# An S4 convolution block with a GEGLU block on one core: first spectrum table on another queue, two activation tables called early, one wider product, and a new order of all steps

## The chip, the cores and the metric

The kernel runs on one core of a Trainium2 chip. The metric is the device time of one execution in microseconds. Before the change it is 791.32 us, the median of 3 runs (790.24 to 792.32).

## The reference, cut to what matters

A sequence of 2048 tokens with 448 channels passes two blocks. The first is a state-space convolution: from the complex parameters A, B, C (448 channels by 256 states) a kernel K of 2048 taps is generated for each channel, and the normalized input is convolved with it. The second is a gated feed-forward block (GEGLU) of width 1792. Both have a layer norm modulated by rows of `silu(c) @ w_mod`.

```python
mod = (_silu(c) @ w_mod).reshape(c.shape[0], 6, 1, -1)       # sa, ca, ga, sb, cb, gb
h = _layernorm(x) * (1 + ca) + sa
# _A_ref: dt = exp(log_dt);  P = exp(dt * A * l);  K = Re(sum_n C * P * dt * B)
#         y = irfft(rfft(K) * rfft(h))[:L] + h * Dskip
x = x + ga * _A_ref(h, ...)
h = _layernorm(x) * (1 + cb) + sb
x = x + gb * (gelu(h @ w_gate) * (h @ w_up)) @ w_down
```

## The kernel before, in words

**Preparation of the taps.** The function `prep(t)` turns 112 channels of A, B and C into two small tables: the logarithm of the magnitude of C*B*dt and of its exponent per tap (`l0`), and the phase (`l1`). It does so in some twenty steps, named `p.A1` to `p.S4` in the code, on [112, 256] tiles. A logarithm (Ln, line 569), an exponential (line 570) and an arctangent (line 580) are among them, all on ScalarE (ACT). Each table is split into three bf16 pieces (`pieces`, lines 527 to 538), written to DRAM (`put`, line 595) and read back transposed in stages of 56 channels (`load_lt`, line 620), tiles `lt`. Tables `ea` and `rd` hold tap numbers. `prep` runs four times, the stage loop eight times.

**Generation.** For each group of 8 channels (`s` = 0 to 55), TensorE (PE) multiplies `lt` with `rd` or `ea` (lines 638, 657, 675), ACT takes exponentials (`mx` line 644, `my` line 662), sines and cosines (`fg`, lines 688, 692, 699), VectorE (DVE) multiplies them (`tx` line 721, `ty` line 725), and PE sums over the states (`kgen`, line 748). Exponentials, sines, logarithm, arctangent and square root each need an activation table in ACT, and an `ACT_TABLE_LOAD` stands in ACT's row wherever the table changes.

**Convolution.** The input is normalized in blocks of 512 tokens (`xt`; statistics lines 877 and 878, scaling line 904) and transformed (`ua` line 921, `ub` line 984) into spectra `us`, kept in DRAM. `k_fft` transforms 160 channels of K at a time, in 11 batches of frequencies: forward product on PE (line 1094, PSUM tile `pf`), product with two u spectra on DVE (lines 1097 and 1098, 3 x 160 elements each; the second spectrum is the first with its halves exchanged), inverse on PE (line 1105). The last 128 channels go through `t_fft`.

**Modulation rows.** `mod_row` (line 800) loads a row of `w_mod` (784 KB) into a buffer of the ring `fg`, which has 4 buffers and also serves the sines, and multiplies it with silu(c) on PE (lines 811 and 815). Three rows are needed at the start, three later.

**Feed-forward block.** Four blocks of 512 tokens: convolution result and norm (`conv_out`), gate and up products (line 1530), down products (lines 1599 and 1630), in fp16 pairs.

**What sets the order.** Every step is a task with a number in the table `PLACE`. The tasks are emitted in the order of these numbers, so each engine's row of instructions, and each DMA queue's, follows from the table. A letter behind a number (a, d, s, p) picks ACT, DVE, SP or POOL where a step can run on several. An engine takes its row strictly in order. SP issues most DMAs; a DMA also waits for the completion of the one eight issues before it, since eight semaphores take turns. In the kernel before, ACT issues the first loads of A, B and C (line 511 for `t` = 0), the two writes of the first table (line 595) and its four reads (line 620). Buffers: 4 of tag `q` for `prep` and `k_fft`, 4 `fg`, 9 `my`, 5 `mx`, 2 `lt`, 2 PSUM tiles `pg`.

Of the kernel before, what the change touches and what calls it, by code (L numbers as in the profile page):

```python
# [40 lines left out]
    "anc": "120 138 145 163 157 200 209 244 266 311 327 339 347 355 438 456 470 487 499 524",  # L41
    "ang": "108 112 126 149 151 169 204 212 241 298 319 324 341 350 421 443 454 476 496 506 511 591 602 610 654 670 690 698 "
        "741 761 764 775 792 795 805 885 894 905 908 927 932 950 1007 1018 1021 1034 1039 1051 1115 1124 1135 1151 1157 1169 "
        "1187 1197",
    "as": "67d 80a 99d 109d 114d 128d 156a 185a 250d 258d 265a 289d 309d 333d 334d 365d",
    "bn": "48 49 60 58 41 50 51 53 227 243 235 239 187 224 197 210",
    "c.ai": "1257",
    "c.ak": "5",
    "c.au": "4",
    "c.c": "2",  # L50
    "c.ea": "20",
    "c.ih": "1283",
    "c.ld": "7",
    "c.rd": "22",
    "c.t1": "219",
    "co.adde": "1329 1347 1366 1355",
    "co.addl": "1384 1387 1421 1410",
    "co.addx": "1495 1510 1499 1522 1676 1716 1739 1688 1799 1811 1817 1809",
    "co.ca": "1404a 1408a 1456a 1441a",
    "co.cb": "1415d 1416a 1459a 1448a",  # L60
    "co.h0": "1398a 1403a 1447d 1430a",
    "co.h2": "1534a 1579a 1571a 1561a 1752a 1748d 1759a 1765d 1856d 1889a 1841a 1873a",
    "co.l0": "1402 1405 1449 1434",
    "co.l2": "1541 1584 1573 1576 1753 1754 1763 1766 1857 1893 1851 1884",
    "co.mme": "1321 1341 1336 1346",
    "co.mml": "1381 1382 1409 1407",
    "co.mmx": "1492 1506 1494 1509 1640 1703 1735 1649 1792 1805 1812 1796",
    "co.n": "1392 1399 1438 1425",
    "co.nx": "1527 1574 1548 1532 1749 1746 1751 1764 1829 1875 1837 1870",
    "co.rc": "1390 1397 1431 1423",  # L70
    "co.rcx": "1525 1743 1828",
    "co.rt": "1388 1393 1424 1418",
    "co.rtx": "1524 1741 1818",
    "co.xt": "1541 1584 1573 1576 1753 1754 1763 1766 1857 1893 1857 1884",
    "co.ta": "1401 1406 1453 1436",
    "co.tb": "1411 1413 1454 1439",
    "cos": "523 609 623 635 689 694 715 708 760 774 794 791 804 819 817 893 906 912 930 946 949 963 1016 1028 1040 1050 1057 "
        "1066 1129 1134 1155 1175 1180 1196 1207 1220",
    "cos2": "124 146 147 167 165 207 213 254 273 321 332 342 349 359 445 462 485 492 502 531",
    "d.hi": "1566 1547 1583 1496 1533 1600 1504",  # L80
    "d.ld": "1555 1538 1569 1484 1516 1585 1491",
    "d.lo": "1567 1552 1587 1501 1535 1602 1514",
    "d0": "13",
    "dn": "1603 1605 1607 1613",
    "dn.k0": "1742 1891 1994",
    "dn.k2": "1755 1896 2000",
    "dn.k3": "1757 1899 2002",
    "dn.r": "1606 1608 1614 1634",
    "dn.r1": "1745 1963 2008",
    "dn.r4": "1768 1903 2004",  # L90
    "dn.r5": "1770 1909 2010",
    "dn.r6": "1778 1908",
    "dn.rh": "2005 2012 2016",
    "dn.s0": "2015",
    "dn.s1": "2017",
    "dn.st": "1657 1658 1620 1639 1747 1780 1775 1779 2007 1952 1950 1948 2014 2006 2013",
    "dn0": "1726 1737 1880 1885 1986 1992",
    "dn1": "1738 1887 1993",
    "dn2": "1767 1902 2003",
    "dn3": "1772 1905",  # L100
    "dn3h": "2009 2011",
    "dn4": "1750 1897 1999",
    "dn5": "1744 1894 1998",
    "dn6": "1761 1898 2001",
    "dsk": "178",
    "dt": "26",
    "e.f": "1666 1718 1704 1615 1650 1628 1685",
    "e.hi": "1668 1720 1708 1617 1653 1631 1689",
    "e.ld": "1656 1705 1696 1610 1638 1619 1675",
    "e.lo": "1671 1723 1710 1618 1655 1636 1691",  # L110
    "ev.end": "1253",
    "ev.fp": "707",
    "ev.geg": "1445",
    "ev.pq": "1328",
    "ev.ps": "1437",
    "ev.ub": "389",
    "ev.w0": "1339",
    "f.fc": "714 716 754 773 801 823 851 880 895 917 942 1015 1030 1052 1071 1094 1114 1137 1158 1189",
    "f.fwd": "738 753 783 806 832 855 879 902 924 947 969 998 1014 1036 1055 1077 1098 1120 1141 1162 1209 1216",
    "f.inv": "750 768 796 815 847 865 889 911 936 960 983 1010 1026 1046 1067 1089 1108 1130 1154 1176 1226 1232",  # L120
    "f.pr": "743 759 790 812 839 859 884 907 931 953 975 1002 1020 1041 1060 1083 1101 1125 1149 1167 1212 1225",
    "f.st": "763 782 809 830 897 878 904 929 977 1000 1009 1023 1042 1079 1090 1106 1131 1148 1168 1193 1243 1240",
    "f.ut": "710 721 755 776 803 826 854 870 901 918 944 966 988 1017 1032 1054 1073 1097 1123 1138 1160 1182",
    "f.z": "758a 778d 802a 829a 868a 871d 896d 926a 952d 979a 1005d 1019a 1038d 1061a 1085a 1102a 1128d 1143a 1163a 1188a "
        "1235a 1239a",
    "gs": "70 110",
    "gu": "1480 1497 1511 1519 1528 1539 1549 1560 1570 1578 1596 1616 1622 1632 1644 1651 1660 1669 1678 1686 1694 1706 "
        "1712 1721 1777 1781 1784 1798 1800 1808 1816 1822 1830 1838 1843 1852 1859 1869 1907 1910 1913 1919 1924 1931 1935 "
        "1941 1945 1958 1964 1970 1974 1981",
    "gu.g": "1429 1450 1458 1465 1468 1471 1474 1481 1502 1508 1521 1529 1540 1550 1562 1572 1581 1595 1604 1623 1633 1641 "  # L130
        "1654 1661 1670 1679 1687 1695 1709 1713 1722 1727 1782 1785 1793 1801 1806 1813 1824 1831 1839 1844 1853 1860 1874 "
        "1878 1911 1914 1920 1925 1932 1936 1942 1946 1959 1965 1972 1975 1982 1987",
    "gu.h0": "1475 1485 1515 1536 1557 1580 1599",
    "gu.ha": "1626 1647 1663 1682 1698 1717 1730 1787 1804 1819 1835 1849 1864 1882 1917 1933 1943 1953 1967 1977 1989",
    "gu.hs": "1629 1646 1667 1690 1701 1732 1734 1794 1820 1826 1846 1862 1871 1888 1923 1930 1955 1957 1983 1979 1996",
    "gu.l0": "1478 1488 1517 1544 1558 1582 1601",
    "gu.la": "1635 1648 1672 1684 1700 1725 1733 1789 1825 1834 1855 1854 1866 1883 1918 1939 1956 1961 1968 1984 1990",
    "gu.ls": "1630 1652 1673 1693 1702 1740 1736 1797 1821 1840 1850 1865 1872 1890 1929 1940 1971 1960 1995 1980 1997",
# [16 lines left out]
    "lt0": "55 136 317 358 568 766 860 955",  # L155
    "lt1": "87 173 335 393 696 833 971 995",
    "m.cp": "532d 589a 818d",
    "m.cp0": "40d",
    "m.ev": "63 68 47 545 598 838",
    "m.ld": "6 19 12 423 539 727",  # L160
    "m.mm": "45 57",
# [1672 lines left out]
```

## Time and profile before

| what | value |
|---|---|
| median of 3 runs | 791.32 us (790.24 to 792.32) |
| the profiled execution's own time | 787.92 us |
| its span, first to last instruction | 786.1 us |
| PE busy | 728.7 us (93%) |
| DVE busy | 591.4 us (75%) |
| ACT busy | 460.1 us (59%) |
| POOL busy | 9.0 us |
| mean granted clock of PE | 0.991 |
| DMA, mean over the span | 178 GB/s |

The span is cut into 40 slices of 19.65 us in the page; a digit is the busy share of a slice in tenths. A row of a timeline has its start, its duration, the engine, the source line, the operation, the tile written and the tile read; in brackets stands how long the engine was idle before it, and what it waited for. Names such as SPq and ACTq stand for an engine's sequencer, which issues DMAs beside the engine's arithmetic. Line numbers are those of the kernel before; the changed kernel's are higher by 2 from line 434 on, by 4 from `prep` on, by 5 behind its arctangent, and by 4 again behind line 1097.

### The profile page before, as it was taken

The numbers are of one execution on the slowest core, as the hardware profiler recorded it, in microseconds if no ns is written. First come the engines' busy times: TensorE is split into PE (matmuls) and PEld (weight loads), VectorE is DVE, ScalarE is ACT, GpSimd is POOL, SyncE is SP. The second block draws the span as 40 slices with busy tenths as digits, with TensorE's granted clock in tenths as the row PEclk, the third lists the DMA queues.
The fourth block names the chain that finished last, engine by engine and source line by source line (L and its number), as shares of the span: only waits on it lengthen the run. The fifth ranks groups of instructions, "written<-read, shape, count | busy, mean of one in ns | idle before, by whom it ended". The sixth has DMA issues, their size and how long they took to land.

```text
span 786.1 us, 19037 instructions
## 1 busy us (share of the span) xinstructions
PE 728.7 (93%) x8166; PEld 445.2 (57%) x8166; DVE 591.4 (75%) x891; ACT 460.1 (59%) x613; POOL 9.0 (1%) x24
## 2 busy tenths in 40 slices
PE   1876889998899999989999999999999999999998
PEld 0333454543667767778784445444595446944478
DVE  4889999999999999988768851469773587134743
ACT  5699999899999999961554730233421244012320
POOL 0000000000000000000300000000000000000000
PEclk9899999999999999999999999999999999999999
DMA  9555558997887767999797884345437324012201
GB/s 265 157 156 145 155 140 249 277 277 227 240 259 216 224 190 216 285 300 251 192 312 221 274 219 146 129 134 186 161 67 213 104 94 134 14 48 94 82 2 60
DMA packets 103791, 139.88 MB, mean 178 GB/s; under 512 B 34388, under 2 KB 85268, under 8 KB 103706
## 3 DMA queue, kind: packets, MB, share of 16 engines
q1 hardware_dynamic: 97828, 130.47, 56.7%
q10 hardware_dynamic: 5318, 7.22, 2.9%
q8 instruction: 64, 1.05, 0.5%
q0 software_dynamic: 560, 0.98, 0.4%
q14 instruction: 21, 0.17, 0.1%
HBM read 100.39 MB, written 36.01 MB: 174 GB/s over the span
## 4 chain that ended last, share of the span: by engine, by line
PE 67%; ACT 13%; DVE 9%; DMA 7%; issue 3%; SPq 1%; ACTq 0%; DVEq 0%
PE pq L1530 29%; PE pq L1630 9%; PE pd L1599 4%; PE kg L748 3%; PE pf L1105 3%; PE pg L675 3%; ACT my L662 2%; DVE ty L725 2%; PE pf L1094 2%; ACT fg L688 2%; PE pq L1524 2%; PE kg L771 2%; DMA yi<-y 2%; PE pd L1630 2%; PE pf L984 1%
## 5 line engine op out<-in xcount | busy, mean ns | idle before, releaser
L1530 PE MATMUL pq<-ht,wr 128*128 128x512 f16 (+1 forms) x1200 | 248.3, 365 | 0.1
L1530 PEld LDWEIGHTS <-wr 128*128 128x128 f16 x1200 | 114.7, 98 | 128.4 <-issue 11.3
L725 DVE TENSOR_TENSOR ty<-my,fg 128x2048 f32<-128x2048 f32 x56 | 127.6, 2285 | 0.9 <-ACT fg L699 0.3
L1537 ACT ACTIVATE ge<-pq 128x512 f32<-128x512 f32 (+1 forms) x60 | 33.9, 566 | 106.4 <-PE pq L1524 71.2
L1544 DVE TENSOR_TENSOR fq<-ge,pq 128x512 f32<-128x512 f32 (+1 forms) x60 | 39.0, 649 | 73.0 <-PE pq L1530 46.1
L1556 ACT ACTIVATE hh<-fq 128x1024 f16<-128x1024 f32 (+1 forms) x49 | 46.7, 961 | 63.9 <-DVE fq L1544 45.3
L721 DVE TENSOR_TENSOR tx<-mx,fg 128x1024 f32<-128x1024 f32 x56 | 67.7, 1219 | 1.8 <-ACT fg L692 1.0
L1630 PE MATMUL pq<-d,hh 128*128 128x224 f16 x476 | 68.9, 259 | 0.0
L748 PE MATMUL kg<-ty,tx 128*32 128x64 f32 x3584 | 62.5, 221 | 4.0 <-issue 2.3
L748 PEld LDWEIGHTS kg<-ty,tx 128*32 128x32 f32 x3584 | 53.0, 110 | 22.7 <-issue 14.7
L1559 DVE TENSOR_TENSOR hlo<-fq,hh 128x1024 f16<-128x1024 f32 (+1 forms) x49 | 53.7, 1106 | 12.9 <-ACT hh L1556 12.7
L1630 PE MATMUL pq<-d,hlo 128*128 128x224 f16 x238 | 61.6, 259 | 0.0
L688 ACT ACTIVATE fg<-pg 128x1024 f32<-128x1024 f32 x56 | 58.1, 1038 | 0.8 <-PE pg L675 0.4
L662 ACT ACTIVATE my<-pg 128x1024 f32<-128x1024 f32 x56 | 55.9, 1032 | 2.6 <-PE pg L657 2.2
L1630 PEld LDWEIGHTS <-hh 128*128 128x128 f16 x560 | 54.2, 98 | 0.9 <-issue 0.2
L1105 PE MATMUL pf<-q,fc 128*128 128x160 f32 x264 | 41.5, 307 | 1.2 <-DVE q L1098 1.2
L692 ACT ACTIVATE fg<-fg,small 128x1024 f32<-128x1024 f32 x36 | 41.5, 1170 | 0.1
L1105 PEld LDWEIGHTS pf<-q,fc 128*128 128x128 f32 x264 | 36.4, 190 | 6.6 <-issue 1.5
L675 PEld LDWEIGHTS <-lt 64*128 64x128 bf16 x304 | 17.9, 95 | 39.0 <-issue 27.0
L675 PE MATMUL pg<-ea,lt 64*128 64x512 bf16 x152 | 30.7, 391 | 8.4 <-ACT fg L699 3.2
L1747 ACT ACTIVATE d<-fq 128x896 f16<-128x896 f32 x14 | 13.2, 946 | 41.7 <-PE pd L1599 27.3
L984 PE MATMUL pf<-ui,fu 128*128 128x448 f32 x66 | 31.0, 575 | 1.9 <-ACT uo L480 1.4
(209 smaller groups left out, 1122.6 us busy)
## 6 DMA issues: line engine op xcount, KB each, us to landing
wr<-w_d SPq DMA_DIRECT2D x21, 896.0 KB
fc<-in_k_fc SPq DMA_DIRECT2D x20, 576.0 KB
u_d<-so SPq DMA_DIRECT2D x32, 224.0 KB
ui<-u_d SPq DMA_DIRECT2D x10, 672.0 KB
fq<-in_wd SPq DMA_DIRECT2D x14, 448.0 KB
w<-in_wgu SPq DMA_DIRECT2D x11, 512.0 KB
us<-uo SPq DMA_DIRECT2D x22, 240.0 KB
q<-us SPq DMA_DIRECT2D x22, 240.0 KB
```

The costliest lines, as they stand in the source:

```text
L662: A.activation(yb.tile.rearrange("p h (n k) -> p n h k", n=2), pb.tile.rearrange("p (n h k) -> p n h k", n=2, h=2), AF.Exp)
L675: T.matmul(pa[:, nh * 512:nh * 512 + 512], w, x, start=(k == 0), stop=(k == 2))
L688: A.activation(fb.tile[:, 0].rearrange("p x (n k) -> p n x k", n=2), pb.tile.rearrange("p (n x k) -> p n x k", n=2, x=2), AF.Sin, scale=TW ...
L692: A.activation(fb.tile[:, 1], fb.tile[:, 1], AF.Sin, scale=-TWO_PI, bias=halfpi)
L721: V.tensor_mul(tx.tile, xb.tile[:, xm, None, :].to_broadcast([128, 2, 512]), fb.tile[:, :, 0])
L725: V.tensor_mul(ty.tile, yb.tile[:, :, None, :].to_broadcast([128, 2, 2, 512]), fb.tile[:, None, :, 1].to_broadcast([128, 2, 2, 512]))
L748: T.matmul(kg[32 * g:32 * g + 32, 2 * (s % 2) + q, :64], tx[:, r, nh, 4 * q + g], ty[:, 0:4:3, nh, 4 * q + g] if r else ty[:, 1:3, nh, 4 * ...
L1105: T.matmul(pz.tile[:, e % 32 - sl0], fc.tile[:, i, 1 + t], pp.tile[:, t, i], start=(t == 0 and e != 32), stop=(t == 1 and e != 0))
L1530: T.matmul(pb.tile[k][:, ts], wr.tile[:, 4 * lo + t, k, c0:c0 + 128], ht[:, m, ts], start=f % 2 == 0 and i == 0, stop=f % 2 == 1 and i == 9)
L1556: A.activation(hg.tile[0][:, cb, c], fq.tile[:, c], AF.Copy)
L1559: V.tensor_sub(hg.tile[1][:, cb, c], fq.tile[:, c], hg.tile[0][:, cb, c])
L1630: T.matmul(bank(k)[:, m], x[:, p, q[0], ts], w[:, p, q[1]], start=new and m == 0 and p == 0 and z == 0, skip_group_check=True, stop=i in ( ...
```

## The change

It has five parts.

1. The writes and reads of the first table (`put`, `load_lt` for the first stage) are issued by SP and no longer by ACT.
2. In `prep` the logarithm is written to `x(7)`, not over `x(10)`. It so no longer waits for the load of the second half of A, B, C (`L3` is the buffer of that load). The step `p.B2` reads `x(7)`, and `p.E1`, which overwrites `x(7)`, now waits for `p.B2`.
3. Two one-element activations are added, a logarithm behind the first exponential (`pre.ln`) and an arctangent behind the step `p.S3` of the first `prep` (`pre.at`). The table loads that belong to them stand there in ACT's row.
4. In `k_fft` one DVE instruction multiplies both u spectra with the K spectrum, which is read twice by a broadcast: 22 instructions of 960 elements in place of 44 of 480.
5. `PLACE` has new numbers for all tasks.

```diff
-    "c.ld": "7",
+    "c.ld": "8",
...
+    PRE_LN = add("pre.ln", {"ACT": 0.2}, -8.4, lambda: A.activation(dump, eps, AF.Ln), [t_dt], table=LN)
...
-        S2 = op("S2", {"ACT": 0.28}, lambda: A.activation(x(10), x(3), AF.Ln), [B1, L3], LN, k=0.6)
-        S3 = op("S3", {"ACT": 0.28}, lambda: A.activation(x(2), x(10), AF.Exp, scale=0.5), [S2], EXP, k=0.65)
+        S2 = op("S2", {"ACT": 0.28}, lambda: A.activation(x(7), x(3), AF.Ln), [B1, PRE_LN if t == 0 else None], LN, k=0.6)
+        S3 = op("S3", {"ACT": 0.28}, lambda: A.activation(x(2), x(7), AF.Exp, scale=0.5), [S2], EXP, k=0.65)
...
+        pre_at = add("pre.at", {"ACT": 0.2}, v0, lambda: A.activation(dump, eps, AF.Arctan), [S3], table=ATAN) if t == 0 else None
...
-        B2 = op("B2", {"ACT": 0.28}, lambda: A.activation(x(10), x(10), AF.Identity, scale=0.5, bias=ld[:, t:t + 1]), [S2, S3], k=0.7)
+        B2 = op("B2", {"ACT": 0.28}, lambda: A.activation(x(10), x(7), AF.Identity, scale=0.5, bias=ld[:, t:t + 1]), [S2, L3], k=0.7)
...
-        S4 = op("S4", {"ACT": 0.28}, lambda: A.activation(x(5), x(5), AF.Arctan), [D1], ATAN, k=1.0)
+        S4 = op("S4", {"ACT": 0.28}, lambda: A.activation(x(5), x(5), AF.Arctan), [D1, pre_at], ATAN, k=1.0)
...
-        E1 = op("E1", {"DVE": 0.66}, phase, [S4, G1], k=1.1)
+        E1 = op("E1", {"DVE": 0.66}, phase, [S4, G1, B2], k=1.1)
...
-                (adma if t == 0 else dma)(lh_d[t, e, :, :6], lb.tile)
+                dma(lh_d[t, e, :, :6], lb.tile)
...
-                (adma if sc == 0 else dma)(
+                dma(
...
-            for t in range(2):
-                V.tensor_mul(pp.tile[:, t, :ne], ut.tile[:, t, :ne], pk.tile[:, :ne])
+            V.tensor_mul(pp.tile[:, :, :ne], ut.tile[:, :, :ne], pk.tile[:, None, :ne].to_broadcast([128, 2, ne, n]))
```

What the new numbers do is seen in the rows of the engines. The first place is SP's queue at the start of the program, before (`xt` are the input tokens, `ld` and `c_sb` the small vectors log_dt and c, `fg` a row of w_mod, `q` the parameters A, B, C of the next `prep`, `au` and `ak` stage matrices):

```order
1 L486 DMA c_sb<-in_c 112x4
2 L486 DMA au<-in_k_au 128x128
3 L486 DMA ak<-in_k_ak 128x256
4 L805 DMA fg<-in_w_mod 112x1792
5 L486 DMA ld<-in_A_log_dt 112x4
6 L852 DMA xt<-in_A_u 128x1792
7 L805 DMA fg<-in_w_mod 112x1792
8 L852 DMA xt<-in_A_u 128x1792
9 L805 DMA fg<-in_w_mod 112x1792
10 L486 DMA ea<-in_k_ea 128x1536
11 L486 DMA rd<-in_k_rd 128x1025
12 L511 DMA q<-in_abc 112x1024
```

The same place in the changed kernel:

```order
1 L857 DMA xt<-in_A_u 128x1792
2 L488 DMA ld<-in_A_log_dt 112x4
3 L488 DMA c_sb<-in_c 112x4
4 L810 DMA fg<-in_w_mod 112x1792
5 L857 DMA xt<-in_A_u 128x1792
6 L810 DMA fg<-in_w_mod 112x1792 x2
7 L600 DMA lh_d<-lh 112x1536
8 L488 DMA au<-in_k_au 128x128
9 L488 DMA rd<-in_k_rd 128x1025
10 L515 DMA q<-in_abc 112x1024
11 L625 DMA lt<-lh_d 64x7x128 x2
12 L488 DMA ea<-in_k_ea 128x1536
```

The first block of tokens now comes first, the write of the first table (`lh_d`) stands ahead of `au`, `rd`, the next parameters and `ea`, its two first reads (`lt`) ahead of `ea`, and `ak` comes later than is shown.

The second place is ACT's row at the start, before (`small` is a column of constants; the rows of line 511 are DMAs that ACT issues):

```order
1 L511 DMA q<-in_abc 112x1024
2 L511 DMA q<-in_abc 112x512
3 L551 ACT_TABLE_LOAD
4 L551 ACTIVATE q<-q 112x512
5 L552 ACTIVATE q<-q 112x256
6 L569 ACT_TABLE_LOAD
7 L569 ACTIVATE q<-q 112x256
8 L570 ACT_TABLE_LOAD
9 L570 ACTIVATE q<-q 112x256
10 L577 ACTIVATE q<-q,ld 112x256
11 L494 ACTIVATE dts__106<-ld 112x4
```

and in the changed kernel:

```order
3 L496 ACT_TABLE_LOAD
4 L496 ACTIVATE dts__106<-ld 112x4
5 L497 ACTIVATE dts__106<-dts__106 112x4
6 L500 ACT_TABLE_LOAD
7 L500 ACTIVATE small<-small 128x1
8 L568 ACTIVATE q<-q,dts__106 112x256
9 L569 ACTIVATE q<-q 112x256
10 L555 ACTIVATE q<-q 112x512
11 L556 ACTIVATE q<-q 112x256
12 L573 ACTIVATE q<-q 112x256
13 L582 ACTIVATE q<-q,ld 112x256
14 L797 ACT_TABLE_LOAD
```

The exponential of log_dt (`dts`), which needs the vector `ld`, moved from behind the logarithm to the front of the row, the table of the logarithm is loaded behind it, and the logarithm itself (line 573) has no table load of its own any more; the table of exponentials is loaded again behind it.

The third place is DVE's row at the start of the changed kernel; before, the product of line 542 (now 546) was the first row behind the two memsets:

```order
3 L882 BN_STATS st<-xt 128x6
4 L883 BN_AGGR mv<-st 128x2
5 L882 BN_STATS st<-xt 128x6
6 L883 BN_AGGR mv<-st 128x2
7 L546 TENSOR_TENSOR q<-q 112x1024
8 L551 TENSOR_TENSOR q<-q 112x256
9 L552 TENSOR_TENSOR q<-q 112x256
```

Two blocks of token statistics moved ahead of the first product of A, B and C.

Counted over all rows of the phase of generation, the letters in the table move single steps between ACT and DVE. To DVE go three bf16 pieces (`lh`), one copy of a K spectrum's rows (`ako`) and two further copies; to ACT go three copies of `zo` of 480 elements, three copies of `ke`, one absolute value of 1024 elements (`fg`) and one further copy. ACT has 42 table loads in place of 43, and two added activations of one element. In the feed-forward block four splits of `hl` (two instructions each) move from ACT to DVE.

The three later loads of w_mod rows stand at 462, 564 and 749 in the table (423, 539 and 727 before), and their products on PE at 503, 576 and 773 (527, 581 and 772 before).

More of the change, by code (lines that the diff above doesn't have):

```diff
@@ L594, in go @@
             def go():
-                (adma if t == 0 else dma)(lh_d[t, e, :, :6], lb.tile)
-            return add("p.put%d" % e, {"ACT" if t == 0 else "SP": 0.42}, v0 + dv * k, go, dep, use=[lb], kb=344)
+                dma(lh_d[t, e, :, :6], lb.tile)
+            return add("p.put%d" % e, {"SP": 0.42}, v0 + dv * k, go, dep, use=[lb], kb=344)
         PUT[t] = (put(0, l0, [P0], 1.1), put(1, l1, [P1], 1.7))
@@ L619, in go @@
             for nh in range(2):
-                (adma if sc == 0 else dma)(
+                dma(
                     b.tile[64 * nh:64 * nh + 64, e],
                     lh_d[t, e, c0:c0 + 8 * SUBS, :, 128 * nh:128 * nh + 128].rearrange("(s c) q n -> (c q) s n", c=8))
-        q = {"ACT": 1.3} if sc == 0 else {"SP": 0.9}
+        q = {"SP": 0.9}
         e0 = add("lt0", q, v, lambda: go(0), [PUT[t][0], PAD[t]], [b], kb=299)
```

440 rows, old and new, of the table PLACE are left out of this document.

## Prediction

> **What bounds the kernel now.** I read the page's busy slices first, then a table by stage, then the chain of waits and the timeline of the first 46 us.
>
> ```profile
> span 786.1 us, 19037 instructions
> PE   1876889998899999989999999999999999999998
> DVE  4889999999999999988768851469773587134743
> ACT  5699999899999999961554730233421244012320
> ```
>
> The kernel has three parts. In the first two or three slices no arithmetic engine is full. Up to slice 17 DVE and ACT are both full, with PE close behind. From slice 18 on PE is full to the end. The table by stage gives sizes; its columns are PE, PEld, DVE, ACT and POOL busy, the granted clock, the DMA engines' share and GB/s.
>
> ```profile
> 0.00:20.00 20.00, 2.55 (x9) 0.73 (x10) 9.85 (x24) 10.60 (x18) 1.52 (x11) 1.00 0.91 263
> 20.00:40.00 20.00, 16.32 (x50) 7.65 (x50) 17.17 (x39) 13.13 (x19) 0.00 (x0) 0.87 0.55 163
> 60.00:80.00 20.00, 13.08 (x272) 7.35 (x271) 19.76 (x33) 19.90 (x26) 0.00 (x0) 0.98 0.51 149
> 120.00:140.00 20.00, 18.43 (x275) 8.82 (x276) 19.84 (x27) 17.52 (x28) 0.00 (x0) 1.00 0.88 248
> 320.00:340.00 20.00, 18.39 (x469) 13.34 (x472) 20.00 (x19) 18.65 (x24) 0.00 (x0) 1.00 0.96 300
> 480.00:500.00 20.00, 20.00 (x108) 10.18 (x106) 5.49 (x10) 0.95 (x1) 0.00 (x0) 1.00 0.07 20
> ```
>
> In the first 40 us ACT lacks 16.3 us and DVE 13.0 us of work. From 60 to 340 us each is between 88 and 100% busy in the stages shown, so time there is saved only by work taken off them or by better packing. In the last part PE shows no gap: what the change moves there (four splits of `hl`) lies beside PE's work and costs nothing while PE has 20.00 of 20; if that cover were gone, four splits would be about 2 us, each a cast like `lh` below (0.41) and a small one. So the change is decided at the start and in the generation.
>
> The chain of waits says what the start waits for, and gives the price of transfers.
>
> ```profile
> 0.75 4.65 DMA q<-in_abc
> 18.52 7.48 DMA lh_d<-lh
> 97.35 3.25 DMA u_d<-so
> 121.03 8.37 DMA fg<-in_w_mod
> ```
>
> The parameters land at 5.4 us, `prep` runs to 18.5, and the write of the first table then takes 7.48 us. A write of 224 KB in a later, quieter stage takes 3.25. The difference is explained by the DMA engines, which are full from about 3 us until 25 us:
>
> ```profile
> 6.00:8.00 2.00, 0.00 (x0) 0.00 (x0) 1.41 (x3) 1.28 (x2) 0.00 (x0) 1.00 1.11 310
> 24.00:26.00 2.00, 2.00 (x5) 0.98 (x5) 1.97 (x5) 0.63 (x1) 0.00 (x0) 1.00 0.71 275
> ```
>
> **Part by part: the start.** These are the rows of the timeline on which the first term rests.
>
> ```profile
> 5.42 1.22 DVE L542 TENSOR_TENSOR q<-q 112x1024 f32<-112x1024 f32 x1 [4.51 <-DMA q<-in_abc]
> 7.47 0.63 ACT L551 ACTIVATE q<-q 112x512 f32<-112x512 f32 x1 [0.72 <-DVE q L548]
> 9.17 1.28 ACT L569 ACT_TABLE_LOAD   x1 [0.76 <-DVE q L558]
> 10.46 0.42 ACT L569 ACTIVATE q<-q 112x256 f32<-112x256 f32 x1
> 13.10 1.75 DVE L574 RECIPROCAL q<-q 112x256 f32<-112x256 f32 x1
> 16.44 1.72 PE L811 MATMUL pf<-fg,c_sb 112*32 112x448 f32 x8 [16.44 <-DMA fg<-in_w_mod]
> 20.79 8.13 PE L815 MATMUL pf<-fg,c_sb 112*128 112x448 f32 x16
> 26.09 1.36 ACTq L620 DMA_DIRECT2D lt<-lh_d  x2
> 28.85 0.09 PEld L638 LDWEIGHTS <-lt 64*128 64x128 bf16 x1 [0.65 <-DMA lt<-lh_d]
> 31.26 1.02 ACT L644 ACTIVATE mx<-pg 128x1024 f32<-128x1024 f32 x1
> 43.66 1.02 ACT L688 ACTIVATE fg<-pg 128x1024 f32<-128x1024 f32 x1
> ```
>
> The mark that I follow is the first exponential of the generation, at 31.26, and the first sine, at 43.66.
>
> *Arrival.* ACT's first step now waits for `ld`, which stands behind 896 KB of `xt` on SP's queue, and DVE's first step waits for `xt` itself. At best they land as the parameters do now, at 5.4. At worst they wait for all of the first loads, 896 KB of tokens, 672 KB of parameters and 224 KB of ones: 1792 KB at 310 GB/s is 5.9 us, from about 2 us on, so 7.9. I take 7.0, between the two and nearer the late end.
>
> *Chain of the first table.* ACT: `dts` 0.4, table of the logarithm 1.28, the dummy 0.2, line 564's two steps 0.9, ready at 9.8. DVE: two token statistics at about 0.8 (0.615 below and a short aggregate), then 2.1 for lines 542 to 548 as now (5.42 to 7.47): 10.7. Squares, sizes and the logarithm took from 7.47 to 9.17 and then 0.42; without the table load the logarithm ends at 12.8. Then line 577 (0.5), the table of exponentials 1.28, two small steps 0.6: 15.2, where it is 12.6 now (10.46, 0.42, another load of 1.28 and 0.42). The three steps around the reciprocal take 2.6: 17.8. The arctangent table lies under them, so the arctangent follows at once and takes 0.4, to 18.2. The bf16 pieces of the first table need the tail of ACT's row and two subtractions, 2.2 together: the write is issued at about 20.0 (17.8 and 2.2), 1.5 us later than now.
>
> *What it meets.* At 18.52 the write finds ahead of it the parameters, ones, two token blocks, three w_mod rows, and besides them `au`, `ak`, `ea`, `rd` and the next parameters, 1280 KB in all, at 310 GB/s worth 4.1 us. Of these all but `ak`, which comes much later, now stand behind it. 7.48 less 4.1 is 3.4, close to the quiet 3.25. So I take 3.3 and the write lands at 23.3, not 26.0. The reads follow with the 2.76 us that they take now (26.09 to 28.85), plus 0.5 for `au`, `rd` and parameters that go between: 26.6.
>
> *What comes last then.* ACT must first bring in the modulation rows and the square root. PE's chain for the rows starts when silu(c) is there, about 16.1 (16.44 now); 4.1 (half of 8.13), 1.7, 4.1 and 1.0 for the sum over rows (two of the sixteen) give 27.0, then one copy of 0.5 and a table load of 1.28: the first exponential at 28.8 in place of 31.26, **2.5 us earlier**. Here PE's chain and no longer the table comes last, which is why the 2.25 us by which the table is early and the loads of the two tables are not all kept. ACT's own stand on the reads (at 26.09, and the wait ahead of it) is gone, since SP now holds them; queued behind SP's waits are the next parameters and `ea`, and `ea` is needed only at the second kind of product of the stage. The second table, which ACT reads now behind its first exponentials, goes the same way and is earlier too, so it doesn't hold the sine: I carry 2.5 us to the first sine. Ends: 4 if the first loads land at 5.4, 0.5 if the chain of the first table is 2 us later than worked out.
>
> The Trainium skill, page "DMA: Bandwidth & Descriptors", section "Issuing engines are not separate DMA queues", says that DMAs from all issuing engines run on the same 16 DMA engines and interleave, and that issuing from several saves only issue time. By this rule the change of queue alone leaves the write at 7.48 us, and only the order of what stands ahead can help; the full DMA shares above agree with it, and it speaks for the first rival.
>
> The skill's page "ScalarE: Activation LUTs", section "What ACT_TABLE_LOAD costs", gives 1283 ns for the load and a drain of about 1380 ns more. The rows show 1.28 us and the logarithm 0.01 us behind it, so no drain; by the page a load that is taken off the path would be worth 2.66 us.
>
> **Part by part: the generation.** These groups carry the second term (busy us, mean ns).
>
> ```profile
> L725 DVE TENSOR_TENSOR ty<-my,fg 128x2048 f32<-128x2048 f32 x56 | 127.6, 2285 | 0.9 <-ACT fg L699 0.3 <-ACT fg L692 0.3 <-issue 0.2
> L721 DVE TENSOR_TENSOR tx<-mx,fg 128x1024 f32<-128x1024 f32 x56 | 67.7, 1219 | 1.8 <-ACT fg L692 1.0 <-ACT fg L699 0.9
> L1098 DVE TENSOR_TENSOR q<-q,pf 128x480 f32<-128x480 f32 x44 | 26.7, 648 | 1.2 <-PE pf L1094 1.0
> L877 DVE BATCH_NORM_STATS2 st<-xt 128x6 f32<-128x448 f32 x16 | 9.8, 615 | 0.0
> L683 DVE TENSOR_SCALAR fg<-pg 128x1024 int32<-128x1024 int32 x6 | 7.3, 1220 | 0.9 <-PE pg L675 0.9
> L680 ACT ACTIVATE fg<-pg 128x1024 f32<-128x1024 f32 x30 | 30.8, 1035 | 0.9 <-DVE ke L766 0.7
> L482 DVE COPY zo<-pf 128x480 f32<-128x480 f32 x7 | 4.6, 653 | 0.5 <-PE pf L1105 0.5
> L480 ACT ACTIVATE zo<-pf 128x480 f32<-128x480 f32 x13 | 7.6, 588 | 0.0
> L482 DVE COPY ke<-kg 128x252 f32<-128x252 f32 x17 | 7.0, 412 | 0.2
> L480 ACT ACTIVATE ke<-kg 128x252 f32<-128x252 f32 x11 | 4.3, 393 | 4.1 <-PE kg L748 4.1
> L482 DVE CAST lh<-q 112x512 bf16<-112x512 f32 x7 | 2.8, 412 | 0.0
> L480 ACT ACTIVATE lh<-q 112x512 bf16<-112x512 f32 x9 | 5.8, 639 | 6.6 <-DVE q L589 2.4 <-DVE q L536 2.4 <-DVE sig L795 1.8
> ```
>
> *The product.* Lines 721 and 725 differ by 1024 elements and 1066 ns, so 1.04 ns an element; 960 elements would take 1219 less 64 x 1.04, 1152 ns. Two of 480 take 26.7/22 = 1.21 us of DVE. That is 0.06 us for each of 22 batches, 1.4 us in all.
>
> *The letters.* ACT: three pieces less (-1.92), three `zo` (+1.76), three `ke` (+1.18), one `fg` (+1.04), two copies less and one more (-0.6), one table load less (-1.28), two dummies (+0.4): 0.6. DVE: +1.24 -1.96 -1.24 -1.22 and about +0.7 for the copies: -2.5, with the product -3.9. ACT gets nothing off and DVE 3.9 of some 290 us. Since either engine can come last, a stretch gains only where DVE does. I take **1.0 us** of the 3.9; the ends are -1 (ACT last throughout) and 3.9.
>
> *The new order* in this stretch has no row that prices it. ACT lacks 2.5 us in the stage from 120 to 140, where a w_mod row sits in one of four `fg` buffers from 121.03 until its product (104 steps of the table later; now 41). A shorter stay can give up to 2.5 back, and other waits can come; I take nothing, with 3 us either way as an estimate from that one stage's shortfall.
>
> **The sum.** Against the profiled execution's own 787.92: 787.9 - 2.5 - 1.0 = 784.4. It lies 3.4 us under the median of 791.32, so against the runs I say 791.3 - 3.5 = **787.8 us**.
>
> **The rivals.** A difference below 0.3%, 2.4 us, can't be told from no change here.
>
> *The start is given back.* The engines become full 2.5 us earlier, but a later transfer sets the pace, so the first stall, such as the stage from 120 us on, takes up the gain. For it: the DMA share is 0.88 to 0.96 there, and these bytes are not fewer. Against it: DVE is at 19.84 in that stage, so what is done ahead of it counts. It gives 789 to 793, say 790.5.
>
> *The later w_mod rows hold PE up*, the rival on the other side. The loads for the second and the third late row stand only 12 and 24 steps ahead of their products in the table. Step 423 was reached at 121.03, so a step is 0.286 us: leads of 3.4 and 6.9 us against 8.37 that such a load took. PE would stand 5.0 + 1.5 = 6.5 us, ACT and DVE starve behind it, since PE's row is strict and the two `pg` buffers cover only about 2 us. Less the 3.5 gained that is 3.0 slower, 794.3. It decides when SP issues the load less than 8.4 us ahead of the product. Against it: SP has nothing else to do and may run ahead of the table.
>
> *More than forecast.* The shorter stay of the first row gives its 2.5 us back and DVE's 3.9 count in full: 2.5 + 3.9 + 2.5 = 8.9, 782.4.
>
> *The change doesn't do what it says*: the logarithm's table could be loaded twice if another function came between; ACT's row in the order shows none. The middle of this is the first rival's time.
>
> **How the numbers follow.** Forecast 0.45, more 0.12, given back 0.25, PE held up 0.18. Faster by over 0.3% takes the forecast without the share in which the start yields under 2.4 (0.02), and "more": 0.55. The same: 0.02 + 0.25 = 0.27. Slower: 0.18. The range leaves out a part of "more" and of the held-up case: 783.0 to 794.0.
>
> **What would show it.** Right: the first exponential near 28.8 and the first sine near 41.2; the write of the first table landing near 23.3; the logarithm without a table load ahead of it; line 1102 with 22 instructions near 1.15 us; all stages after the start earlier by a growing amount, up to about 3.5 us where the gate products begin. Wrong: the first exponential later than 30.5 (the loads land late), ACT or PE idle for over 2 us in front of a product of `fg` and `c_sb`, or gate products that begin no earlier than now.

## The result, and the profile after

The changed kernel takes 795.84 us (median of 16 runs, 790.38 to 802.60), the kernel before 789.56 (16 runs, 786.29 to 792.32). The ratio is 1.0086, 95% interval 1.0068 to 1.0104: **slower by 0.86%**, where I forecast 787.8 us. The ratio leaves out the run of 802.60 us, the only one in a slow state, and is not the quotient of the two medians (1.0080). The profiled execution of the changed kernel took 792.80 us (span 791.0) and lies 3.0 us under its median, that of before took 787.92 and lies 1.6 under its own. So the two profiles differ by 4.9 us and the runs by 6.3: the profile shows the loss a little too small.

These are the slices of the changed kernel's page. PE has an 8 and a 7 in slices 20 and 22 (376 to 396 and 415 to 435 us), where it had 9, and ends on 7 in place of 8.

```profile
PE   1776889999999999999897999999999999999997
DVE  5899999999999999979665853378872787135653
ACT  5699999999999999943542730143421342013320
```

**The start.** The timeline of the changed kernel, DVE's first statistic, ACT's first step, the write and the reads of the first table on SP, PE's first use of the table, the first exponential and the first sine; below them a row of the table by 2 us (PE, PEld, DVE, ACT, POOL, clock, DMA share, GB/s):

```profile
7.59 0.63 DVE L882 BATCH_NORM_STATS2 st<-xt 128x6 f32<-128x448 f32 x1 [6.68 <-DMA xt<-in_A_u]
9.30 0.21 ACT L496 ACTIVATE dts__106<-ld 112x4 f32<-112x4 f32 x1 [6.34 <-DMA ld<-in_A_log_dt]
21.40 0.32 SPq L600 DMA_DIRECT2D lh_d<-lh  x1
24.31 1.35 SPq L625 DMA_DIRECT2D lt<-lh_d  x2
30.11 0.28 PE L643 MATMUL pg<-rd,lt 64*128 64x256 bf16 x1 [2.75 <-DMA lt<-lh_d]
31.02 2.86 ACT L649 ACTIVATE mx<-pg 128x1024 f32<-128x1024 f32 x3 [1.78 <-PE pg L643]
43.06 1.94 ACT L693 ACTIVATE fg<-pg 128x1024 f32<-128x1024 f32 x2
...
20.00:22.00 2.00, 2.00 (x5) 0.97 (x3) 1.97 (x5) 1.31 (x3) 0.00 (x0) 1.00 0.00 0
```

The first exponential is at 31.02, not at the forecast 28.8 (31.26 before), the first sine at 43.06 (43.66 before). From the write's issue to the reads' issue it is 2.9 us now, where it was 7.57 (18.52 to 26.09). But from the reads' issue to PE's first use 5.8 us pass, where 2.76 passed, and PE waits 2.75 us. The last row shows why that need not be: from 20 to 22 us no DMA moves at all. SP stands at the table's write, and behind it in SP's row stand `au`, `rd` and the next parameters (768 KB, issued from 21.76 to 22.80) and `ea` (issued at 25.71), which then run into the write and the reads.

**The generation.** The merged product has the length that I worked out (1152 ns). The first product of the last transforms marks the generation's end, the first row of before, the second of the changed kernel:

```profile
354.78 1.60 PE L1189 MATMUL pf<-ako,fc 128*128 128x128 f32 x12 [0.70 <-ACT ako L480]
```

```profile
L1102 DVE TENSOR_TENSOR q<-q,pf 128x960 f32<-128x960 f32 x22 | 25.2, 1147 | 2.4 <-PE pf L1099 2.4
...
349.35 1.60 PE L1193 MATMUL pf<-ako,fc 128*128 128x128 f32 x12 [0.70 <-ACT ako L482]
```

It ends 5.4 us earlier in this execution. That is more than the 3.5 that I forecast for start and generation together, though the start gave nearly nothing (0.24 us at the first exponential, 0.6 at the first sine).

**Behind the generation** the gain is lost and more. PE's waits from 340 us to the end, the longest of before and then of the changed kernel:

```profile
PE pd L1409 <- DMA yi<-yb_d: 1.0, 1, 1.0
...
PE pd L1409 <- DMA yi<-y: 0.4, 1, 0.4
```

```profile
PE pd L1413 <- DMA yi<-y: 4.0, 1, 4.0
PE pd L1413 <- DMA y<-lh: 2.8, 1, 2.8
PE pq L1694 <- DVE xn L1701: 2.3, 1, 2.3
```

There are three places. In order of time they are the wait of 2.8 us (at 378 us, for block 0's `yi`), that of 4.0 (at 416 us, for block 1's `yi`) and that of 2.3 (at 781 us, for the last block's half result). PE's timeline shows what they cost; before first, then the changed kernel:

```profile
392.44 2.34 PE L1530 MATMUL pq<-ht,wr 128*128 128x256 f16 x20
...
418.58 0.44 PE L1409 MATMUL pd<-yi,ai 128*64 128x128 f32 x4 [0.36 <-DMA yi<-y]
...
420.04 4.49 PE L1530 MATMUL pq<-ht,wr 128*128 128x512 f16 x20
...
431.08 8.81 PE L1530 MATMUL pq<-ht,wr 128*128 128x512 f16 x40
```

```profile
389.54 2.35 PE L1534 MATMUL pq<-ht,wr 128*128 128x256 f16 x20
...
419.78 0.70 PE L1413 MATMUL pd<-yi,ai 128*64 128x128 f32 x4 [3.96 <-DMA yi<-y]
420.23 1.31 PE L1408 MATMUL pd<-yi,ai 128*64 128x320 f32 x4
...
422.44 5.48 PE L1534 MATMUL pq<-ht,wr 128*128 128x512 f16 x20
...
434.48 8.81 PE L1534 MATMUL pq<-ht,wr 128*128 128x512 f16 x40
```

The gate products begin 2.9 us early (389.54 against 392.44), so 2.5 of the 5.4 went in the transition up to there; the longer first wait (2.82 against 1.04 us) is 1.8 of them. Forty products of 512 columns behind the second wait the same work begins 3.4 us late (434.48 against 431.08): 6.3 us went there. Of these the longer wait is 3.6 us, and 2.2 go by between its end and the last row, at a lower granted clock: twenty gate products take 5.48 us where they took 4.49, and the first `yi` products 0.70 where they took 0.44. About 0.9 comes back until 760 us, and the third wait takes 2.4: -5.4 + 2.5 + 6.3 - 0.9 + 2.4 = +4.9, the difference of the spans.

*Why `yi` of block 1 is late.* The chain of waits of the changed kernel names the store that it waits for, and ACT's queue what stands ahead of that store:

```profile
396.50 13.14 DMA y<-zo
410.38 9.27 DMA yi<-y
```

```profile
395.56 0.85 ACTq L1363 DMA_DIRECT2D w_d<-wr  x2
...
396.50 0.52 ACTq L1235 DMA_DIRECT2D y<-zo  x1
```

Two stores of split weights (`wr.sa`, 896 KB each) go out together, right ahead of the last stores of `y`. Before, the first went out at 388.42 and the second at 396.34, behind ACT's last `y` at 393.83. ACT's is not the only late store: POOL's last `y`, which waits for DVE's `zo`, is issued at 399.20 (393.26 before) and takes 10.3 us, so both land near 409.6. No run here moves POOL's store alone. The table of stretches (before, then changed) shows the rest:

```profile
388.00:396.00 8.00, 7.42 (x75) 5.87 (x74) 7.72 (x21) 6.22 (x13) 0.69 (x1) 1.00 0.91 301
396.00:416.00 20.00, 20.00 (x177) 15.42 (x176) 12.26 (x26) 11.31 (x20) 0.00 (x0) 1.00 1.01 287
416.00:424.00 8.00, 7.64 (x45) 3.40 (x44) 6.57 (x12) 3.02 (x5) 0.00 (x0) 1.00 0.99 302
```

```profile
388.00:396.00 8.00, 8.00 (x78) 6.41 (x77) 6.15 (x16) 6.59 (x12) 0.00 (x0) 1.00 0.10 39
396.00:416.00 20.00, 19.64 (x157) 13.18 (x154) 12.32 (x23) 8.60 (x14) 0.69 (x1) 1.00 0.98 304
416.00:424.00 8.00, 4.22 (x18) 1.99 (x19) 2.24 (x5) 0.85 (x1) 0.00 (x0) 0.60 1.03 306
```

The DMA share is the last column but one. The stretch from 396 to 416 is full in both. But ahead of it the DMA engines were 91% busy before, and are 10% busy now: some 6.5 us of transfers (0.81 of 8 us) are missing from this stretch, and the full one, at whose end PE waits, has to take them. And the last row has the clock: 0.60 in the stretch with the wait, 1.00 before.

*The end.* DVE's row, the changed kernel with PE's wait beneath it; before, DVE made the half result (line 1697, now 1701) at 776.62, ahead of the three-step result of `dn.r5`:

```profile
781.08 0.62 DVE L1644 TENSOR_TENSOR xn<-xn,pq 128x448 f32<-128x448 f32 x1 [2.02 <-PE pq L1634]
...
782.94 0.38 DVE L1701 TENSOR_TENSOR xn<-pq,rows 128x224 f32<-128x224 f32 x1
...
783.37 0.35 PE L1694 MATMUL pq<-d,hh 128*128 128x224 f16 x2 [2.33 <-DVE xn L1701]
```

PE's last 42 products need the bank that the half result reads. In the new order that result stands behind three steps which themselves wait for the product just ahead.

### The profile page after: what moved, and what is told of

The parts are those of the page before. It is cut to its first block, busy times and chain, and to the rows that moved or that the text cites. A ratio compares the mean times of both kernels' runs of the same rounds, so it can differ in the third digit from the quotient of the medians.

```text
span 791.0 us, 18984 instructions
## 1 busy us (share of the span) xinstructions
PE 728.0 (92%) x8166; PEld 443.7 (56%) x8166; DVE 592.3 (75%) x877; ACT 455.2 (58%) x606; POOL 9.1 (1%) x24
## 4 chain that ended last, share of the span: by engine, by line
PE 48%; DMA 4%; DVE 2%; issue 1%; ACT 0%; POOL 0%; SPq 0%; ACTq 0%; DVEq 0%
PE pq L1534 28%; PE pq L1634 9%; PE pd L1603 4%; PE pq L1528 2%; DMA y<-zo 2%; PE pd L1634 2%; DMA yi<-y 1%; PE pd L1408 1%; DMA yb_d<-z 1%; DVE my L1204 1%; PE pd L1413 1%; PE pf L1211 1%; DVE q L1204 0%; DMA y<-lh 0%; POOL yi L1301 0%
## 5 line engine op out<-in xcount | busy, mean ns | idle before, releaser
L753 PE MATMUL kg<-ty,tx 128*32 128x64 f32 x3584 | 60.9, 220 | 4.1 <-DVE tx L726 1.7
L693 ACT ACTIVATE fg<-pg 128x1024 f32<-128x1024 f32 x56 | 58.4, 1050 | 1.7 <-ACT uo L482 1.0
L685 ACT ACTIVATE fg<-pg 128x1024 f32<-128x1024 f32 x31 | 32.8, 1062 | 0.2 <-ACT zo L482 0.2
```

Source lines behind the costliest of these rows:

```text
L693: A.activation(fb.tile[:, 0].rearrange("p x (n k) -> p n x k", n=2), pb.tile.rearrange("p (n x k) -> p n x k", n=2, x=2), AF.Sin, scale=TW ...
L753: T.matmul(kg[32 * g:32 * g + 32, 2 * (s % 2) + q, :64], tx[:, r, nh, 4 * q + g], ty[:, 0:4:3, nh, 4 * q + g] if r else ty[:, 1:3, nh, 4 * ...
```

## Experiments

My theory after the result: the generation gained, and three places of the new order behind it lose more. The rivals: the losses belong to the gain (a transfer or the weights set the pace there in any order), or the bytes and not their order decide. The table's numbers may be fractions in these kernels; nothing else is changed where only numbers are shown. e1 to e4, e5 to e8 and e9 to e12 were each measured together with the kernel before on one chip (its medians are 789.44, 788.92 and 788.82 us), and ratios are to that.

### The whole new order behind the generation

e3 keeps the changed kernel up to the generation's end; every step that stood at 1253 or later in the old table follows the old order (and so do `f.st` 21, `t.fd` 6 and 7).

> The changed kernel up to the end of the generation, and from there to the end the order of the kernel before (its numbers for every step from 1253 on; three late steps of the transforms follow it too). Theory A (the new order behind the generation costs all of the loss, and the generation's gain of about 5.4 us at 349 us is real and carries to the end): 4.5 to 5.5 us faster than the kernel before, near 784 us. Theory B (the gain is lost in the transition whatever its order, because a transfer or the weights set its pace): within 1.5 us of the kernel before.

Measured: 783.9 us, ratio **0.9925 (0.9911 to 0.9939)**, 5.5 us faster than before. PE's waits behind the generation, and its end:

```profile
PE pd L1383 <- DMA yi<-y: 1.3, 1, 1.3
PE pd L1383 <- DMA yi<-yb_d: 0.9, 1, 0.9
...
350.35 1.60 PE L1163 MATMUL pf<-ako,fc 128*128 128x128 f32 x12 [0.70 <-ACT ako L452]
```

Theory A holds: the generation's gain (4.4 us in this execution) comes through to the end, so the whole loss, 11.9 us by the medians and 12.7 by the ratios (1.0086 less 0.9925), is the order behind it.

### The second wait: stores of weights

e1 puts both stores behind ACT's last store of `y`, e5 puts the first where the DMA engines were empty.

```diff
 e1
-wr.sa: 1440 1439
+wr.sa: 1450.4 1450.5     (ACT's t.st[6] is at 1450)
 e5
+wr.sa: 1404.5 1450.5     (behind w.la[0] at 1404)
```

> The changed kernel, with the two ACT stores of split weights (w_d<-wr, 896 KB each, issued at 395.56 us) put behind the ACT store of y (y<-zo, 192 KB, issued at 396.50, landing 13.14 us later). Theory A (the queue's order: the last store of y stands behind 1.8 MB of weights, and the load of block 1's yi waits for it): y<-zo lands in 4 to 6 us, PE's wait of 3.96 us for yi at 415.8 and the low clock behind it are gone, and the kernel is 4 to 6 us faster than the changed one, near 790 us. Theory B (the bytes: the DMA engines are full from 400 to 424 us whatever the order, and yi comes when all of them have gone through): yi lands no more than 1 us earlier, and the time stays within 1.5 us of the changed kernel's 795.8.

Measured: 792.5 us, ratio 1.0031 (1.0011 to 1.0052). Its row of PE and its chain:

```profile
418.73 0.44 PE L1415 MATMUL pd<-yi,ai 128*64 128x128 f32 x4 [0.41 <-DMA yi<-y]
...
401.07 10.03 DMA y<-zo
```

The wait fell from 3.96 to 0.41 us, and the time by 3.3 us by the medians (4.3 by the ratios), just under or in theory A's 4 to 6. But A's account by ACT's queue is not enough: the last store to land is now the one on POOL's queue, issued at 401.07, and it takes 10.03 us though no weights stand on that queue. (When ACT's store lands the profile doesn't tell.) The weights were issued at 397.2 and 397.8 on ACT's queue, so what stands ahead in time seems to count, on whatever queue. The Trainium skill, page "DMA: Bandwidth & Descriptors", section "Issuing engines are not separate DMA queues", says that DMAs issued by different engines run on the same 16 DMA engines and interleave; POOL's store agrees with it (10.03 us here, 4.8 in the kernel before).

> The changed kernel, with the first store of split weights (w_d<-wr, 896 KB) put on ACT's queue behind the weight loads, where the DMA engines stand empty from 389 to 396 us (share 0.21 and 0.00), and the second behind the ACT store of y. Putting both behind the store of y took PE's wait for yi from 3.96 to 0.41 us and left the last store of y, on POOL's queue, at 10.03 us. Theory A (the load of block 1's yi is late because work that could have been moved in the empty stretch is moved together with the stores of y): the POOL store of y takes 5 to 7 us, PE's wait is 0 to 0.5 us, and the time is 3 to 5 us under the changed kernel's 795.8, at most 1.5 us better than with both behind. Theory B (the number of bytes between 396 and 418 us does not matter, only the order of ACT's queue): the same as with both behind, within 0.5 us.

Measured: 789.52 us, ratio **1.0005 (0.9982 to 1.0028)**, 6.3 us under the changed kernel's median. The stretches that were empty and full:

```profile
388.00:396.00 8.00, 8.00 (x74) 6.01 (x73) 5.97 (x17) 5.64 (x11) 0.00 (x0) 1.00 0.64 223
396.00:416.00 20.00, 19.81 (x172) 14.66 (x170) 13.41 (x28) 9.77 (x18) 0.69 (x1) 1.00 0.92 240
```

The empty stretch is used (0.64 in place of 0.10), the full one falls to 0.92, POOL's store takes 7.7 us (10.3 in the changed kernel), and PE's wait for block 1's `yi` is gone from the list. It is some 2 to 3 us better than e1, more than theory A allowed and against B, but the two intervals overlap. So the empty stretch as a cause beside the order of ACT's queue agrees with the rows and is not settled by the times; that the place of these two stores makes the second wait is settled by both runs.

### The third wait: the half result

```diff
-dn.rh: 1999 2002 2005
+dn.rh: 1995.5 2002 2005     (dn.r5[2] is at 1997)
```

> The changed kernel, with the first half-block result of the last block (dn.rh, line 1701) moved ahead of the result in three steps (dn.r5) on DVE, where the kernel before had it. Theory A (this order alone makes PE wait 2.33 us ahead of its last 42 products): the wait is gone and the kernel is 2.3 us faster than the changed one. Theory B (the product would then wait for something else, such as the other bank or the outputs): less than 1 us.

Measured: 792.48 us, ratio 1.0036 (1.0019 to 1.0052), 3.4 us under the changed kernel by the medians, where the row said 2.3. The wait is gone from PE's list. Theory A; the surplus of 1 us is within the two intervals.

### All repairs together

e9 has e5 and e2 in one; e10 adds a repair for the first wait; e11 adds the start's (below).

```diff
 e10
+t.fd 6, 7: 1254.5 1254.6    (were 1393, 1391, behind the early pieces of yi on SP)
+t.inv 7: 1376.5             (was 1387, behind the products with yi of block 0 from 1377)
```

> The changed kernel with both single repairs: the stores of split weights on either side of the stores of y (alone it was at 1.0005 of the kernel before), and the half-block result ahead of the result in three steps (alone 1.0036). The changed kernel is at 1.0086. Theory A (they are separate waits, at 416 us and at 781 us, and add): 1.0086 less 0.0081 less 0.0050, near 0.9955, some 786 us. Theory B (one hides the other, or both share a cause): 0.999 to 1.001.

Measured: 786.43 us, ratio 0.9975 (0.9956 to 0.9994). In us the two give 1.0086 less 0.9975, 8.8 us; the timeline said 6.3 and 2.4, so 8.7. The ratio lies between the two theories: the single repairs sum to 0.0131, some 10.3 us, and 8.8 is 1.5 short of that, which the intervals allow. In the profile both waits are gone, so they are separate; that they add in full is not shown.

> The kernel with both repairs and a third: the loads of the last two batches of transforms (my and fg, moved by the change behind the early pieces of yi on SP's queue) put back to the transition's beginning, and the inverse transform of the eighth batch ahead of the products with yi of block 0 on PE. In the changed kernel PE waits 2.82 us there, at 377.6 us, against 1.04 before, with 4.2 us of inverse transforms behind it in its row. Theory A (this wait is the rest of the loss): the wait is 0 to 1 us, and the kernel is 1.5 to 2.5 us faster than with two repairs, as far as the one with the old order (0.9925). Theory B (the wait only moves to the next thing that the gate products need): less than 0.7 us.

Measured: 785.11 us, ratio 0.9958 (0.9939 to 0.9976). PE's wait in e10:

```profile
386.85 0.44 PE L1419 MATMUL pd<-yi,ai 128*64 128x128 f32 x4 [2.20 <-DMA y<-lh]
```

The inverse transforms do run ahead of it now, and the wait is as long as in e9 (2.3). From the first transforms of the last kind to the gate products it takes 40.0 us in e10, 39.8 in e9 and 37.5 in e3, which has the old order. So the wait only moved: theory B. The 1.3 us between the medians lie within the intervals. What would remove the first wait in the new order, and the 2 us or so that the transition loses with it, stays open; the old order has 1.0 us there.

### Where the generation's gain comes from

e4 is the kernel before with only line 1102's product; e8 is e3 with the product in two instructions again.

```diff
-            for t in range(2):
-                V.tensor_mul(pp.tile[:, t, :ne], ut.tile[:, t, :ne], pk.tile[:, :ne])
+            V.tensor_mul(pp.tile[:, :, :ne], ut.tile[:, :, :ne], pk.tile[:, None, :ne].to_broadcast([128, 2, ne, n]))
```

> The kernel before, with only the product of a K spectrum with both u spectra made one instruction of 960 elements (22 of 1.15 us on DVE in place of 44 of 0.61). Theory A (the product gives what its row says, 0.06 us in each of 22 batches): 0.5 to 1.4 us faster than before, and the generation's gain of 5 to 6 us comes from the new order. Theory B (fewer instructions let DVE and PE pack better): 3 us faster or more.

Measured: 789.38 us, ratio 1.0002 (0.9983 to 1.0021): nothing, below theory A's 0.5, which the interval doesn't exclude, and against B.

> The kernel with the new order up to the generation and the old one behind it (783.9 us), with the product of a K spectrum with both u spectra made in two instructions again. Theory A (the generation's gain of 5 us is the order's, and the product is worth 0.06 us in each of 22 batches or nothing, as it was with the old order): 0 to 1.5 us slower than 783.9. Theory B (the new order was made for the short product, and loses its gain without it): 3 to 5 us slower.

Measured: 785.93 us, ratio 0.9969 (0.9951 to 0.9987). That is 2.0 us above e3 by the medians and 3.5 by the ratios, on either side of the gap between the theories. The new order up to the generation's end, with the changes at the start, gives 0.31% without the short product and 0.75% with it; the product without them gives nothing. The stage from 120 to 200 us shows what the order does, in the kernel before, the changed one, e4 and e8 (third to fifth number: PE, PEld, DVE busy, then ACT):

```profile
120.00:200.00 80.00, 72.74 (x1116) 35.08 (x1113) 77.18 (x99) 75.27 (x102) 0.00 (x0) 0.99 0.91 258
```

```profile
120.00:200.00 80.00, 75.29 (x1188) 35.87 (x1187) 78.86 (x101) 77.61 (x103) 0.00 (x0) 1.00 0.92 265
```

```profile
120.00:200.00 80.00, 73.27 (x1122) 35.26 (x1120) 77.35 (x98) 75.34 (x101) 0.00 (x0) 0.99 0.91 261
```

```profile
120.00:200.00 80.00, 74.34 (x1122) 34.87 (x1120) 77.20 (x100) 76.22 (x100) 0.00 (x0) 1.00 0.90 260
```

The changed kernel has 2.3 us more of ACT and 1.7 more of DVE in this stage than before, the product alone (e4) 0.1 and 0.2 more, the new order without it (e8) 1.0 and 0.0. This agrees with both being needed; one execution of each can't prove it.

### The start

e6 is e3 with `rd`, `au`, the next parameters and `ea` ahead of the first table's write on SP; e7 is e3 with that table's write and reads on ACT's queue again.

```diff
 e6
+c.rd: 46.2   c.au: 46.3   p.ld 2: 46.4   c.ea: 46.5     (p.put0 is at 57)
 e7
+                (adma if t == 0 else dma)(lh_d[t, e, :, :6], lb.tile)      (and the reads likewise)
+p.put0 0: 37.5   lt0 0: 55.5
```

> The kernel with the new order up to the generation and the old one behind it (783.9 us), with four loads on SP's queue (rd, au, the next parameters q, ea, 928 KB) put ahead of the first table's write instead of behind it. In the changed kernel the DMA engines stand empty from 20 to 22 us while SP waits for the table, and the table's reads, issued at 24.31, land at 30.11. Theory A (these loads sit between the write and the reads and hold them up): the reads land at 26.5 to 27.5, the first exponential is bound by the modulation rows and the table load at 29.3 in place of 31.0, and 1 to 1.7 us of that is kept to the end. Theory B (the engines of the generation give it back, or the write itself is then delayed by them): less than 0.5 us.

Measured: 782.69 us, ratio 0.9929 (0.9914 to 0.9944). The stretch that was empty, and the first exponential:

```profile
20.00:22.00 2.00, 2.00 (x4) 0.96 (x3) 1.97 (x5) 1.32 (x3) 0.00 (x0) 1.00 1.04 297
...
29.37 2.85 ACT L623 ACTIVATE mx<-pg 128x1024 f32<-128x1024 f32 x3
```

The four loads are 1152 KB (448 for the parameters), not 928. The first exponential comes at 29.37, where 29.3 was worked out, and without a wait: the modulation rows and the table load are the bound now. From the reads' issue to PE's first use 2.9 us pass, in place of 6.0 in e3. The time is 1.2 us under e3's by the medians, the ratio is no better than e3's; e11 tells more.

> The kernel with the three repairs and with rd, au, the next parameters q and ea ahead of the first table's write on SP's queue. With the old order behind the generation this took the first exponential from 31.7 to 29.4 us and the profiled execution from 782.4 to 780.3, but its ratio was 0.9929 beside 0.9925 without it, on another chip. Theory A (the start's 2.3 us are kept to the end): 1.5 to 2.5 us faster than the three repairs alone. Theory B (the generation gives it back): within 0.7 us of them.

Measured: 782.76 us, ratio 0.9934 (0.9912 to 0.9956), 2.35 us under e10 by the medians on the same chip: theory A by the medians, though the two intervals overlap. The profile of e11 doesn't show all of it: its first exponential is at 30.32 (31.03 in e10), and the reads are issued 4.8 us behind the write, 3.2 in e6. So that the four loads behind the write cost about as much as the start was to gain agrees with the times, and is not shown by this profile alone.

> The kernel with the new order up to the generation and the old one behind it (783.9 us), with the write and the reads of the first table on ACT's queue again (the write behind the last piece that it needs, the reads ahead of the square root). SP then issues rd, au, q and ea without waiting for the table. Theory A (the move to SP's queue is what the forecast said, a gain): the first exponential comes 1 to 2.5 us later than 31.0 and the kernel is 1 us slower. Theory B (what SP holds back behind its wait costs as much as ACT's stand on the queue): the first exponential is at 29.5 to 31 and the time is the same or up to 1 us less.

Measured: 784.95 us, ratio 0.9952 (0.9937 to 0.9967); the first exponential is at 30.55. The first exponential is where theory B has it, ahead of the 31.0 of the changed kernel and the 31.63 of e3 on SP's queue, and the time is theory A's, 1.0 us above e3 by the medians. So the move to SP's queue by itself doesn't bring the first exponential forward, and the 1.0 us of time is not certain, since the two intervals meet; against e6, with the loads ahead of the write, ACT's queue is 2.3 us slower by the medians.

> The kernel with the new order up to the generation, the old one behind it and the four loads ahead of the first table's write, once more, beside the repaired new order on the same chip. Theory A (old and repaired order behind the generation are equal): within 1 us of the kernel with all four repairs. Theory B (some wait of the new order is left): 1 to 3 us faster than that.

Measured: 782.78 us, ratio **0.9928 (0.9908 to 0.9948)**, equal to e11 (782.76): theory A. With e6 and, by its ratio, e3 these are the fastest versions: e11 and e12 lie 6.0 us under the kernel before on the same chip, and by the ratios some 12 under the changed one.

## Why the prediction was wrong

- **What bounds the kernel: this step failed.** I wrote that PE is full from slice 18 on and "shows no gap" in the last part, so that what the change moves there "costs nothing while PE has 20.00 of 20", and took the transition and the end at nothing. I had shown rows from 320 to 340 and 480 to 500, none between. The row of before from 400 to 420, shown below, has 19.64 of PE at a DMA share of 1.02, and PE waited 0.36 us for block 1's `yi`: the load came just in time, at the end of a full stretch. PE full meant that the old order was tight there, not that an order could not hurt. (In e3, with the old order and an earlier generation, this wait is 1.3 us.) The experiments put 8.8 us on two of the three places and some 12 us on the whole order behind the generation.

```profile
400.00:420.00 20.00, 19.64 (x161) 13.52 (x160) 11.20 (x20) 8.00 (x13) 0.00 (x0) 1.00 1.02 272
```

- **The start, -2.5 us: a size failed.** Arrival: DVE's first step at 7.59 as taken (7.0 to 7.9), but ACT's at 9.30, 1.4 later than my latest. The write is issued at 21.40 (20.0 forecast) and the reads at 24.31 (23.3). The term that was mis-sized is the reads: I gave 0.5 us to what stands between, and it costs about 3 (5.8 in place of 2.76; with the loads moved, 2.9 in e6 and 2.7 in e12). So the table came last after all, not PE's rows: the table load ended at 29.24 and the first exponential waited until 31.02. With those loads moved the step comes out at 29.37 (e6), 28.83 (e12) and 30.32 (e11), where I had 28.8.
- **The product: right in length, not in effect.** 1147 ns against 1152. Alone it gives nothing (e4), as part of the new order 2 to 3.5 us (e8).
- **The order in the generation: mis-sized.** I took nothing, with 3 us either way. Seven executions of the same order to the generation's end (the changed kernel, e1, e2, e3, e5, e9, e10) reach it at 349.35 to 354.35, on average 351.5, 3.3 us ahead of the profile of before (and e4, in the old order, reaches it at 355.85). That this is near the 3.5 that I forecast for start and generation together is luck: I had 2.5 of it from the start, which gave 0.24 at the first exponential.
- **The rivals.** The late w_mod rows did not hold PE up: their products run at 143.6, 162.5 and 213.7 us without a wait for a load. "The start is given back" fell with the start's gain itself. "More than forecast" was right for the generation and was hidden by the rest. None of my rivals placed a loss behind the generation, though more than a third of the table's numbers (1253 to 2017) lie there.

## What to carry to other kernels

When a table sets the order, look at every stretch that it renumbers, and above all at the waits that are short now: 0.4 us for a load at the end of a stretch of full DMA is a warning, not a cover. Read the DMA share by a few us and look for an empty stretch right ahead of a full one; a large store moved across that border can cost whoever waits at its end. A queue that stands in a wait holds back everything behind it, so put the loads that don't depend on the wait ahead of it.

## What the hardware showed unexpectedly

- **A wait of PE can cost more than its length.** Behind the wait of 3.96 us twenty products of 512 took 5.48 us in place of 4.49, and the granted clock was 0.60 from 416 to 424 us, where it is 1.00 in e1 and e5, which wait at most 0.41 us there. All in all the 3.6 us of longer wait went with 6.3 of loss. It isn't so behind every wait: for block 0's `yi` PE waits 2.32 us in e9 and 2.57 in e1, and the four products behind take 0.69 us in the first and 0.44 in the second. What decides it no run here shows.
- **The same instructions, different times.** Seven executions of one order differ by 5.0 us at the generation's end. In e10, which is last, PE stopped once for 2.2 us with no releaser in the profile:

```profile
336.26 0.56 PE L1105 MATMUL pf<-ako,fc 128*128 128x160 f32 x2 [2.22 <-issue]
```

- **A 192 KB store took 4.8, 7.7, 10.0, 10.3 or 13.14 us** (POOL's before, in e5, e1 and the changed kernel; ACT's in the changed kernel), where the kernels differ in what had been issued ahead of it, on any queue.
